# FNet mixing and a dropless mixture of experts on one core: the second block's weights requested ahead of both blocks' rows

## The chip, the core and the metric

The kernel runs on one NeuronCore of a Trainium2 chip. The engines are TensorE (PE in the profile, with its weight loads as PEld), VectorE (DVE), ScalarE (ACT), GpSimd (POOL) and SyncE (SP, which issues most DMAs). The metric is the device time of one execution in microseconds. The time before is the median of three executions.

## The reference

Two stages in a row, all in float32.

```python
# x: (8, 2496, 256)
X = np.fft.fft(np.fft.fft(x, axis=1), axis=2).real     # FNet mixing
t = X.reshape(8 * 2496, 256)                           # 19968 tokens
logits = t @ w_gate                                    # 8 experts
e = argmax(logits); g = softmax(logits)[e]             # one expert for each token
y[token] = relu(t[token] @ w1[e]) @ w2[e]              # 256 -> 1024 -> 256
out = g[:, None] * y                                   # every token is computed, none dropped
```

## The kernel before

**Mixing.** The sequence transform of a batch (2496 rows) is done as 104 x 24 points. `first(b)` folds the input tile `xq` on VectorE, multiplies it with the cosine and sine table on TensorE (`half1`, tile `s`), copies the result to `t1` on ScalarE and stores it to a DRAM buffer `Td` (L342). Behind each such store it calls `load` for the following batch (L289). `regroup(b, h)` reads `Td` back in another order (L354). `second(b)` makes the 24-point transform, the transform over the features and the gate's logits, and `route` finds each token's expert and its place in a DRAM buffer `Xs`, in which every expert has a region of its own.

**Scatter.** Twenty groups of 128 rows for each batch are written to `Xs` by indirect DMAs from GpSimd, one for each call of `send` (L470, put on record as L236). A row is 258 floats: 256 features, the token's number and its gate weight.

**Experts.** `todo` is the list of blocks in the order in which they are worked on. The first six blocks have rows of batch 0 alone: two of 256 rows, then four of 128. Which expert a block has, and where its rows start, is known only at run time: `plan` computes a table for each group of blocks (`tabs`), and SP reads the table into a register before it issues the block's DMAs (L531 for the rows, L544 for the expert).

- `fetch_weights` issues two DMAs of 1 MB each, `w1_sb` (L546) and `w2_sb` (L548). Each has three buffers. One of the three buffers of `w1_sb` holds the table `rt` at first, so two are free at the start.
- `fetch_rows` issues five DMAs: four of the features (L536) and a small one of the token numbers and gate weights (L540). They wait for all the scatters of the block's batches.
- `fetch_some(k, most)` keeps `xbs` (rows) and `got` (weights) filled up to three blocks ahead. In each turn of its loop it takes the next rows, if their batch is in `whole`, and then the weights of block `k + len(got)`, but it leaves the loop if that block's table is not in `tabs` yet.

Then a block is transposed on VectorE (`turn`, L584, tile `xT`), multiplied with `w1_sb` (tile `ph`), put through the ReLU, multiplied with `w2_sb` (tile `py`), scaled and scattered to the output. Later blocks use a form with seven half-size products in place of eight.

**Order.** Nothing is scheduled automatically: each engine executes its instructions in the order in which the Python program emits them. `experts` is a generator that yields while it has nothing to emit, and the main loop (L997 on) then emits steps of the mixing of batches 1 and 2, of `close(0)` (the planning) and of `send`. At the start of the first block (L777 to L787) `experts` waits for the first table, fetches the first block's weights (`fetch_some(0, 1)`, L780), yields once so that the main loop emits every scatter that is left and puts batch 0 into `whole`, fetches on (`fetch_some(0)`, L783), yields nine times, during which the main loop emits one step each of planning or mixing, and transposes block 0. `fetch_some(k)` in L788 is called for every block.

In SP's order before, from the first weights on, with the time of issue in the profiled execution: the weights of block 0 (70.20 and 70.75 us), the rows of block 0 (85.08 to 87.59), the rows of block 1 (88.38 to 91.27), the weights of block 1 (92.06 and 92.61), one `Td` store (93.06) and one `xq` load (93.53) of the nine steps, the rows of block 2 (94.91), the weights of block 2 (100.44 and later).

Of the kernel before, what the change touches and what calls it, by code (L numbers as in the profile page):

```python
# [160 lines left out]
def in_order():  # L161


    todo = []
    for b, now in enumerate(rounds()):
        parts = [[(b, size, last, i) for i in range(k)] for size, k, last in now]
        if b == B - 1:
            few, many = parts[-2:]
            sure, more = many[:SURE], many[SURE:]
            k = len(few)  # L170
            end = more[(len(more) + 1) // 2:]
            more = more[:len(more) - len(end)]
            rest = []
            for i in range(k):
                rest += few[i:i + 1] + sure[len(sure) * i // k:len(sure) * (i + 1) // k][:1]
                rest += more[i:i + 1]
                rest += sure[len(sure) * i // k:len(sure) * (i + 1) // k][1:]
            parts = parts[:-2] + [rest + end]
        todo += sum(parts, [])
    return todo  # L180
# [35 lines left out]
def kernel(ctx: ExitStack, tc, x, w_gate, w1, w2, out):  # L216
# [310 lines left out]
    def fetch_rows(b, size, tab, i, flat=None):  # L527


        n = size // 128  # L530
        row = nc.sync.value_load(tab[:, 0, i:i + 1], min_val=0, max_val=ROWS - size)  # L531
        if flat is None:
            xb = bp.tile([128, BIG // 128, W], F32, tag="xb", name="xb", bufs=3)
            flat = xb[:].rearrange("p t c -> p (t c)")
        for q in range(4):
            taken(nc.sync.dma_start(  # L536
                out=flat[32 * q:32 * q + 32, 0:2 * size].rearrange("p (j e) -> p j e", e=64),
                in_=Xs[ds(row, size), 64 * q:64 * q + 64].rearrange("(j k) e -> k j e", k=32)), b)
        meta = flat[:, 2 * size:2 * size + 2 * n].rearrange("p (t c) -> p t c", c=2)
        taken(nc.sync.dma_start(out=meta, in_=Xs[ds(row, size), D:].rearrange("(t p) c -> p t c", p=128)), b)  # L540
        return flat, meta

    def fetch_weights(tab, i):
        ev = nc.sync.value_load(tab[:, 1, i:i + 1], min_val=0, max_val=E - 1)  # L544
        w1_sb = bp.tile([128, 2, F], F32, tag="w1", name="w1_sb", bufs=3)
        nc.sync.dma_start(out=w1_sb[:], in_=w1[ds(ev, 1)].rearrange("o p c f -> p (o c) f"))  # L546
        w2_sb = bp.tile([128, FC, D], F32, tag="w2", name="w2_sb", bufs=3)
        nc.sync.dma_start(out=w2_sb[:], in_=w2[ds(ev, 1)].rearrange("o p c d -> p (o c) d"))  # L548
        return w1_sb, w2_sb
# [28 lines left out]
    def turn(b, size, xb):  # L578


        xT = bp.tile([128, 2, BIG], F32, tag="xT", name="xT", bufs=1)
        n = min(size, 256)
        for h in range(-(-size // 256)):
            vec.transpose(free(xT[:], 256 * h, [32, n // 32], [BIG, 2], [1, 32]),  # L584
                          free(xb, 512 * h, [64, n // 32], [1, 2], [2, 32]))
            odd = xT[:, 1, 256 * h:256 * h + n]
            act.activation(odd, odd, ACTF.Copy, scale=-1.0)  # L587
            yield xT
        if halved(b, size):
            th = size // 2  # L590
            xs = bp.tile([128, 3, th], F32, tag="xs", name="xs", bufs=1)
            r = right(xs, *(xT[:, c, k * th:(k + 1) * th] for c in range(2) for k in range(2)))
            yield r
# [136 lines left out]
    def experts(todo):  # L730
# [4 lines left out]
        xbs, got, xT, used, left, soon, final = [], [], None, None, None, None, {}  # L735
# [15 lines left out]
        def fetch_some(k, most=3):  # L751

            b, size, last, at = todo[-1]
            if "pads" in whole and not final:
                rows = sp.tile([128, NSL, W], F32, tag="rows", name="rows")
                for i in range(3):
                    b, size, last, at = todo[i - 3]
                    final[len(todo) - 3 + i] = fetch_rows(b, size, tabs[b, size, last], at,
                                                          rows[:, i:i + 1].rearrange("p t c -> p (t c)"))
            while max(len(got), len(xbs)) < min(most, len(todo) - k) or len(xbs) < len(got):  # L760
                n = len(xbs)
                b, size, last, at = todo[k + n]
                if k + n in final:
                    xbs.append(final[k + n])
                elif (b, size, last) in tabs and b in whole:
                    xbs.append(fetch_rows(b, size, tabs[b, size, last], at))
                elif n < len(got):
                    break
                b, size, last, at = todo[k + len(got)]
                if (b, size, last) not in tabs:  # L770
                    break
                if len(got) <= n:
                    got.append(fetch_weights(tabs[b, size, last], at))

        for k, (b, size, last, at) in enumerate(todo):
            n, m = size // 128, BIG // size
            if not k:  # L777
                while todo[0][:3] not in tabs:
                    yield 0, False
                fetch_some(0, 1)  # L780
                while b not in whole:
                    yield 0, True
                fetch_some(0)  # L783
                for _ in range(9):
                    yield 0, False
                for xT in turn(b, size, xbs[0][0]):
                    pass  # L787
# [177 lines left out]
    tabs, whole = {}, set()  # L965
    todo = in_order()
# [24 lines left out]
    for k, _ in enumerate(second(0)):  # L991
        if k % 2 == 0:
            next(early, None)
        send()
    work = experts(todo)
    steps = {b: mixed(b) for b in range(1, B)}
    for b in range(1, B):  # L997
# [83 lines left out]
```

## The time and the profile before

| what | value |
|---|---|
| median of three executions | 1260.61 us (1259.76 to 1261.67) |
| the profiled execution's own time | 1258.56 us |
| its span, first to last instruction | 1256.8 us |
| mean granted TensorE clock over the span | 0.976 of full speed |
| TensorE matmuls | 1208.1 us busy, 96% of the span |
| TensorE weight loads | 1076.3 us, 86% |
| VectorE, ScalarE, GpSimd | 60%, 34%, 36% |
| DMA | 249.79 MB, mean 199 GB/s over the span |

All times inside the execution count from the first instruction. About 1.8 us of the execution's own time lie outside the span. The page cuts the span into 40 slices of 31.4 us. Matmuls are pipelined and their ends are modelled, so a busy TensorE is one that has work, not one at its peak. The chain of waits follows the work that ended last backwards, step by step, to what released it. The table of DMA queues lists a hardware queue (q1, the DMAs that SP issues) and a software queue (q0, GpSimd's indirect DMAs); both are served by the same 16 DMA engines.

### The profile page before, as it was taken

How to read it: one execution, taken by the hardware profiler on the slowest of the kernel's cores; microseconds unless marked ns; L12 is line 12 of the kernel's file. 1: busy time of each engine (PE TensorE's matmuls, PEld its weight loads, DVE VectorE, ACT ScalarE, POOL GpSimd, SP SyncE). 2: the span in 40 equal slices, each digit the busy share in tenths (PEclk: the TensorE clock that was granted, in tenths of full speed). 3: DMA queues.
4: the chain of work that ended last, by engine and by line, in shares of the span. 5: the costliest groups of instructions: out<-in, count | busy, mean ns of one | idle time of the engine just before them, and what ended most of it. 6: DMA issues, size and time to landing. Idle time of an engine off the chain costs nothing.

```text
span 1256.8 us, 22295 instructions
## 1 busy us (share of the span) xinstructions
PE 1208.1 (96%) x7289; PEld 1076.3 (86%) x7289; DVE 759.6 (60%) x1804; ACT 431.3 (34%) x1167; POOL 447.5 (36%) x527
## 2 busy tenths in 40 slices
PE   5759999999999999999999999999999999999997
PEld 3648998777788899888988899889999999999996
DVE  3455434343456788566866578686888784444653
ACT  1424332333243433434343333442333332222222
POOL 0154527054117522472226603472364241111112
PEclk6869999999999999999999999999999999999998
DMA  8859899873548434673336435453347237878787
GB/s 235 261 174 350 308 317 311 221 237 122 154 153 263 151 110 163 184 234 116 102 124 211 138 96 162 138 180 101 106 139 206 94 105 284 277 285 284 280 292 284
DMA packets 163216, 249.79 MB, mean 199 GB/s; under 512 B 118601, under 2 KB 130227, under 8 KB 143516
## 3 DMA queue, kind: packets, MB, share of 16 engines
q1 hardware_dynamic: 146327, 203.28, 50.7%
q0 software_dynamic: 15888, 42.14, 9.1%
q10 hardware_dynamic: 885, 2.94, 0.7%
q8 instruction: 59, 0.97, 0.3%
q14 instruction: 57, 0.47, 0.1%
HBM read 194.91 MB, written 54.83 MB: 199 GB/s over the span
## 4 chain that ended last, share of the span: by engine, by line
PE 82%; DVE 9%; DMA 4%; ACT 2%; issue 2%; POOL 0%; SPq 0%; POOLq 0%; DVEq 0%; ACTq 0%
PE py L221 25%; PE ph L221 13%; PE a L221 11%; PE c L221 9%; PE p L221 6%; PE b L221 6%; PE d L221 5%; PE e L221 4%; PE s L221 3%; DMA xq<-in_x_dram 1%; DVE xT L584 1%; DMA Td<-t 1%; DVE y L684 1%; DMA Xs<-rows,pi 1%; DVE hT L639 1%
## 5 line engine op out<-in xcount | busy, mean ns | idle before, releaser
L236 POOL DMA_INDIRECT out_dram<-y,ro x163 | 161.4, 990 | 625.3 <-ACT y L680 301.3
L221 PE MATMUL py<-w_sb,hT 128*128 128x256 f32 x1504 | 339.5, 379 | 0.0
L221 PEld LDWEIGHTS py<-w_sb,hT 128*128 128x128 f32 x1504 | 281.4, 190 | 36.9 <-issue 1.0
L236 POOL DMA_INDIRECT Xs<-rows,pi x160 | 162.4, 1015 | 112.0 <-DVE rows L410 56.7
L221 PE MATMUL ph<-xT,w_sb 128*128 128x128 f32 (+2 forms) x992 | 171.1, 328 | 11.2 <-DVE xT L584 11.1
L221 PEld LDWEIGHTS ph<-xT,w_sb 128*128 128x128 f32 x992 | 136.3, 192 | 35.1 <-issue 16.8
L410 DVE SCALAR_TENSOR_TENSOR rows<-p,zs 128x129 f32<-128x129 f32 x160 | 48.9, 348 | 128.8 <-ACT lg L408 124.8
L221 PE MATMUL a<-xT,w_sb 128*128 128x256 f32 (+1 forms) x512 | 117.8, 357 | 0.0
L838 DVE TENSOR_SCALAR hT<-ph 128x512 f32<-128x512 f32 x43 | 29.7, 691 | 123.7 <-PE ph L221 63.7
L587 ACT ACTIVATE xT<-xT 128x256 f32<-128x256 f32 (+1 forms) x94 | 36.5, 388 | 179.2 <-DVE xT L584 140.8
L221 PEld LDWEIGHTS a<-xT,w_sb 128*128 128x128 f32 x512 | 88.6, 190 | 9.7
L892 ACT ACTIVATE y<-py,xb 128x256 f32<-128x256 f32 x94 | 44.6, 475 | 152.2 <-PE py L221 152.2
L636 DVE TENSOR_TENSOR hT<-hT,b 128x512 f32<-128x512 f32 x57 | 39.2, 688 | 75.7 <-PE b L221 50.0
L646 ACT ACTIVATE hT<-a 128x512 f32<-128x512 f32 x57 | 34.0, 597 | 134.1 <-PE a L221 131.1
L221 PE MATMUL s<-xq,w 104*112 104x256 f32 (+2 forms) x208 | 62.8, 425 | 16.3 <-DVE xq L297 12.1
L469 POOL CAST pi<-due 128x1 int32<-128x1 f32 x140 | 45.1, 322 | 65.5 <-ACT due L468 65.5
L221 PE MATMUL a<-w_sb,hT 128*128 128x128 f32 x528 | 66.0, 276 | 0.0
L221 PEld LDWEIGHTS a<-w_sb,hT 128*128 128x128 f32 x528 | 63.1, 192 | 0.7
L221 PEld LDWEIGHTS p<-table,t 120*128 120x128 f32 x352 | 53.6, 202 | 10.6 <-ACT t L372 2.8
L221 PE MATMUL c<-xT,ws 128*128 128x256 f32 (+1 forms) x256 | 60.3, 362 | 1.0 <-DVE hT L642 0.2
L221 PEld LDWEIGHTS s<-xq,w 104*112 104x112 f32 x208 | 38.5, 204 | 26.3 <-DVE xq L297 10.8
L584 DVE STREAM_TRANSPOSE xT<-xb 128x512 f32<-128x512 f32 (+1 forms) x91 | 56.2, 631 | 7.6 <-DMA xb<-Xs 7.6
(149 smaller groups left out, 2072.6 us busy)
## 6 DMA issues: line engine op xcount, KB each, us to landing
w_sb<-in_moe_w_dram SPq DMA_DIRECT2D x132, 1024.0 KB
xq<-in_x_dram SPq DMA_DIRECT2D x24, 896.0 KB
xb<-Xs SPq DMA_DIRECT2D x112, 128.0 KB
Td<-t SPq DMA_DIRECT2D x18, 448.0 KB
t<-Td SPq DMA_DIRECT2D x8, 768.0 KB
t<-Td SPq DMA_DIRECT2D x8, 640.0 KB
xb<-Xs SPq DMA_DIRECT2D x52, 64.0 KB
xb<-Xs SPq DMA_DIRECT2D x88, 32.0 KB
```

The costliest lines, as they stand in the source:

```text
L221: nc.tensor.matmul(o, lhsT=lhsT, rhs=rhs, start=start, stop=stop, **kw)
L236: return unordered(pool.indirect_dma_start(out=dst, out_offset=bass.IndirectOffsetOnAxis(ap=idx, axis=0), in_=rows, in_offset=None, bounds ...
L410: vec.scalar_tensor_tensor(rows[:, k + m, 0:NY], p3[:, 0:NY], zs[:, 0:1], zs[:, 1:], op0=ALU.add, op1=op)
L469: pool.tensor_copy(idx, due[:])
L584: vec.transpose(free(xT[:], 256 * h, [32, n // 32], [BIG, 2], [1, 32]), free(xb, 512 * h, [64, n // 32], [1, 2], [2, 32]))
L587: act.activation(odd, odd, ACTF.Copy, scale=-1.0)
L636: vec.tensor_tensor(h12, h11, b[:], op=add)
L639: vec.tensor_tensor(h21, h12, d[:], op=add)
L646: act.activation(h11, a[:], ACTF.Relu)
L684: vec.tensor_tensor(o, o, p[:], op=add)
L838: vec.tensor_scalar(o, ph[:], 0.0, None, op0=ALU.max)
L892: act.activation(y[:, i % 2], py[:], ACTF.Copy, scale=meta[:, i, 1:2])
```

## The change

One line is added behind the first `fetch_some` call.

```diff
                 while todo[0][:3] not in tabs:
                     yield 0, False
                 fetch_some(0, 1)
+                got.append(fetch_weights(tabs[todo[1][:3]], todo[1][3]))
                 while b not in whole:
                     yield 0, True
                 fetch_some(0)
```

Blocks 0 and 1 have the same table, which is there at this point. SP now issues the two weight DMAs of block 1 directly behind those of block 0, before it waits for the scatters. The numbers of DMAs and of buffers stay the same.

`got` is then one longer when `fetch_some(0)` is called in L783. Its loop takes the rows of block 0 and looks next at the table of block `0 + len(got)`, which is now block 2 and not block 1. That table is finished only within the nine steps that follow, so the loop is left there. The rows of block 1 are fetched by the next call (L788), together with the rows and the weights of block 2. SP's new order is: the weights of blocks 0 and 1, the rows of block 0, the `Td` store and the `xq` load, the rows of block 1, the rows of block 2, the weights of block 2. From there on it is the old one.

## The prediction

> **What bounds the kernel now.** I read the 40 slices first, then the waits of the stretch in which the change acts, then the chain, SP's issues and the DMA view there, and last TensorE's waits in all that follows. The slices say that TensorE is full from the fourth one on:
>
> ```profile
> PE   5759999999999999999999999999999999999997
> DMA  8859899873548434673336435453347237878787
> ```
>
> The third slice (62.8 to 94.3 us) holds the place of the change. Waits between 78 and 93 us (total, times, longest):
>
> ```profile
> PE ph L221 <- DVE xT L584: 11.1, 1, 11.1
> DVE xT L584 <- DMA xb<-Xs: 7.6, 1, 7.6
> ```
>
> TensorE stands still for 11.1 us, until block 0 is transposed, and the transpose waits for block 0's rows. The chain tells what the rows wait for (start, length):
>
> ```profile
> 82.36 2.48 DMA Xs<-rows,pi
> ...
> 86.69 1.98 DMA xb<-Xs
> ...
> 88.79 0.72 DVE xT L584
> 89.51 0.04 issue
> 89.55 3.66 PE ph L221 x8
> ```
>
> The last scatter of batch 0 is issued at 82.36 and lands at 84.84; then SP issues the rows (85.08), they land, are transposed, and TensorE starts at 89.55. So 89.55 - 84.84 = 4.71 us lie behind the last scatter's landing. The weights do not stand in this chain. SP's issues:
>
> ```profile
> 70.75 0.37 SPq L548 DMA_DIRECT2D w_sb<-in_moe_w_dram  x1
> 85.08 1.92 SPq L536 DMA_DIRECT2D xb<-Xs  x4
> 87.19 0.40 SPq L540 DMA_DIRECT2D xb<-Xs  x1
> 88.38 2.29 SPq L536 DMA_DIRECT2D xb<-Xs  x4
> 90.87 0.40 SPq L540 DMA_DIRECT2D xb<-Xs  x1
> 92.06 0.37 SPq L546 DMA_DIRECT2D w_sb<-in_moe_w_dram  x1
> ```
>
> The stages around it (length; busy us of PE, PEld, DVE, ACT, POOL with counts; clock, DMA share, GB/s):
>
> ```profile
> 76.00:78.00 2.00, 1.50 (x12) 1.42 (x13) 1.03 (x4) 1.09 (x6) 1.39 (x3) 1.00 0.99 392
> 78.00:80.00 2.00, 0.49 (x4) 0.27 (x3) 0.80 (x5) 0.65 (x3) 1.70 (x2) 1.00 0.79 305
> 80.00:82.00 2.00, 0.00 (x0) 0.00 (x0) 1.21 (x4) 0.00 (x0) 1.70 (x2) 1.00 0.19 68
> 92.00:94.00 2.00, 2.00 (x13) 1.79 (x11) 0.00 (x0) 0.75 (x2) 0.00 (x0) 0.76 0.53 75
> ```
>
> Block 0's weights fill the DMA engines until about 79 us; from 80 on they are nearly idle. In the DMA view of 79.3 to 85.0 only the software queue is left, and between 100 and 130 us, where the hardware queue is never empty, a scatter takes far longer to land (last number, median us):
>
> ```profile
> q0 software_dynamic: 213, 0.52, 25.7%
> Xs<-rows,pi POOLq DMA_INDIRECT x13, 7.0
> ```
>
> From 93 us to the end TensorE waits for no transfer at all. Its list has six entries, 4.9 us together, the largest being
>
> ```profile
> PE p L221 <- ACT t L372: 2.0, 4, 0.8
> PE p L221 <- ACT t L321: 1.2, 3, 0.7
> ```
>
> So whatever shifts the restart at 89.55 shifts the end by as much, and a transfer that comes sooner behind it has almost nothing to win.
>
> **What the Trainium skill says.** "DMA: Bandwidth & Descriptors", section "Issuing engines are not separate DMA queues": DMAs of SP, ScalarE and GpSimd run on the same 16 engines and interleave. The trace agrees: 2.48 us for the last scatter on quiet engines, 7.0 on full ones. Same page, "Queues, rings and completion order": each engine goes round-robin between its queues, packet by packet, so a scatter is not simply behind all the weights. The trace agrees in part: of the scatters issued in 70 to 86 us the median landed after 4.9 us, though block 0's weights were ahead. "TensorE: Matmul & The Clock Gate", Part 1: the clock is halved after an idle window of some 3.4 us and is full again after a busy one, and the windows run free of the program. The trace agrees: clock 0.50 at the restart, and 0.76 in 92 to 94 us puts the return at 93.0, 3.4 us after it.
>
> **The change part by part.**
>
> *Weights of block 1, moved forward.* Two DMAs of 1 MB. Between SP's last issue for a block's rows and its next weights lie 0.79 us (91.27 to 92.06), for the reading of the table. So they are issued at 71.12 + 0.79 = 71.9 and 72.5. SP has nothing else to do until the scatters have landed: its 1.7 us cost nothing here, and are saved at 91.3. Their buffers are free, and no hardware-queue traffic is left from earlier (the DMA view of 66 to 71 us lists none), so nothing holds them back. Who needs them is not waiting: block 1's first product is at 116.3, and before they had landed by 100.44, when SP's next weight issue got past its wait for them. **Gain on the path: none.**
>
> *What they meet.* Until 79.3 block 0's weights fill the engines in both versions. Then before there were 0.52 MB of scatters to move; now there are 0.52 + 2.10 = 2.62 MB. In 71.5 to 79.3 both queues together moved 346 GB/s, in 76 to 78 us 392; over 74 to 79, 1.85 MB in 5 us, 370. At 370 this is 7.1 us: all is through at 86.4 (86.0 at 392, 86.9 at 346). Scatters are a fifth of the bytes. Behind block 0's weights the view of 79.3 to 85.0 shows 0.4 us of full rate, the scatters that had stayed behind. I add the same, so the last scatter lands at 86.8 in place of 84.84: **2.0 us later.** Bounds: with an even share for the scatters it has its own 2.5 us plus a few packets' delay, 85.1, **0.3**; if the weights always go first, they alone need 2.10 MB at the 265 GB/s that the hardware queue got in 71.5 to 79.3 (2.07 MB in 7.8 us), until 87.2, and the 0.52 MB follow at 370 in 1.4 us, 88.6; the median of 7.0 us on full engines gives 82.36 + 7.0 = 89.4. So **up to 4.5.** I take neither end, since the weights run dry before 7.0 us are over.
>
> *GpSimd.* Twenty scatters, one each 1.28 us. Its DMAs signal on eight semaphores in turn, so the issue at 82.36 needs the landing of the one of 70.71. The longest landing of the trace up to 131 us is 8.4 us, which gives 79.1: the issues don't move. Beyond 11.6 us they would, a part of the slow case.
>
> *Rows of block 0.* Their issue waits for the last scatter; the weights are through by then or within half a microsecond. The 4.71 us stay.
>
> *Rows of block 1, behind the store and the load.* Five DMAs, moved from 88.4 behind one `Td` store (its data copied by 75.9) and one `xq` load (its buffer's last product ended at 74.5): 1.34 MB, 3.6 us at 370. Issued from about 92 to 95 and landed by 98 at the latest; the next transpose on VectorE is at 106.84. **Nothing**, 9 us of cover; without it, each us would be one on TensorE. The store and the load come some 3 us sooner, and the rows and weights of block 2 no later than before; behind them the order is the old one.
>
> *Relief.* 2.10 MB, 5.7 us of full rate, leave the stretch behind 93, which is full until past 130. TensorE waits for no transfer there. **At best 0.7 us** (its single wait in 99 to 103, for ScalarE, if that came from buffers), likely 0.
>
> *Clock.* TensorE is cold at the restart either way, for the first window that is busy throughout: 3.4 to 6.8 us, whatever the time of restart. In this profile it was 3.4, the least. A later restart in the same grid would stay cold until 96.4: a profile after may show up to 1.7 us more, a median over executions not.
>
> **Sum:** 2.0 + 0 + 0. Against the profiled execution's own time that is 1258.56 + 2.0 = 1260.6, with up to 1.7 for the clock's grid 1262.3. The median of the runs shown is 2.05 above that execution, so I put the same 2.0 on it: 1260.61 + 2.0 = **1262.6 us**.
>
> **The rivals.** (1) *The weights starve the scatters*: 3.7 to 4.5 us, 1265; slower. For it: 7.0 us of landing on full engines. Against: the weights run out at 86 to 87. It decides once the last scatter lands after 87.4. (2) *The scatters get their share*: 0.3 us, 1260.9. For it: round-robin; against: the landing of 4.9 us under only one block's weights. (3) *The relief counts*: the weights fill idle engines at little delay, and the freed 5.7 us behind 93 bring something that the waits don't show, half of it say: 1260.6 + 0.3 - 2.9 = 1258.0; against it, the list without transfers. (4) *The fetch isn't sooner*, held by a buffer or a slot: no difference, 1260.6; but all are free.
>
> **How the numbers follow.** 0.2%, 2.5 us, is about what a measurement of this kernel can tell from no change. My case, 1.2 to 2.9 us (1261.8 to 1263.5): 0.50. Rival 1: 0.27; rivals 2 and 4: 0.17; rival 3: 0.06. Slower: all but a little of rival 1 and three tenths of mine, 0.40. Faster: 0.06. Same: 0.54. The range takes in rivals 1 and 2 and 0.8 us for the spread of medians: 1260.0 to 1265.8.
>
> **What would show it.** In the profile after: SP's four weight issues at 70 to 73; a DMA share near 1 until 86; the chain still through the last scatter, with about 4.4 us to land in place of 2.48; rows at 87; TensorE restarting at 91.5 and its waits behind unchanged. It is wrong if the last scatter lands before 85.2 or after 87.8, if TensorE waits for block 1's rows near 107, or if the time falls.

## The result, and the profile after

| | before | after |
|---|---|---|
| median of 22 executions each | 1259.72 us (1255.78 to 1261.87) | 1261.53 us (1259.95 to 1265.02) |
| ratio after to before, 95% interval | | 1.0020 (1.0012 to 1.0027) |
| the profiled execution's own time | 1258.56 us | 1261.17 us |
| its span, mean granted clock | 1256.8 us, 0.976 | 1259.4 us, 0.977 |

The kernel became a little slower: 1.8 us between the medians, 2.5 us by the ratio (1.5 to 3.4). The interval lies above 1, but the effect is about the size of the 0.2% bound, and the forecast (+2.0 us on the median) is inside it. The 1262.6 us that it came to stood on a median of three executions of the kernel before (1260.61); 22 of them put that median 0.9 us lower.

The profile is read in the order of the prediction. The slices of after (busy tenths in 40 slices) show the old picture, with one tenth less in the first slice, ahead of the change, and in the third:

```profile
PE   4749999999999999999999999999999999999997
DMA  8877899763548535573336435453346328888887
```

Waits of after between 78 and 93 us (total, times, longest):

```profile
PE ph L221 <- DVE xT L584: 12.6, 1, 12.6
DVE xT L584 <- DMA xb<-Xs: 9.1, 1, 9.1
```

They are the same two waits, each 1.5 us longer (11.1 and 7.6 before). The chain of after through that stretch (start, length):

```profile
82.02 4.09 DMA Xs<-rows,pi
86.36 0.35 SPq L536
...
87.96 1.93 DMA xb<-Xs
89.98 0.72 DVE xT L584
90.74 3.78 PE ph L221 x8
```

The last scatter is issued 0.34 us *earlier* than before (82.02, not 82.36), but takes 4.09 us to land in place of 2.48. From landing (86.11) to restart (90.74) there are 4.63 us; before they were 4.71. So from the last scatter's issue to TensorE's restart it is 8.72 us in place of 7.19, which is 1.53 us more, all of it in that one landing. SP's issues in after:

```profile
70.43 0.37 SPq L548 DMA_DIRECT2D w_sb<-in_moe_w_dram  x1
71.59 0.34 SPq L546 DMA_DIRECT2D w_sb<-in_moe_w_dram  x1
72.11 0.33 SPq L548 DMA_DIRECT2D w_sb<-in_moe_w_dram  x1
86.36 1.92 SPq L536 DMA_DIRECT2D xb<-Xs  x4
...
91.89 2.12 SPq L536 DMA_DIRECT2D xb<-Xs  x4
...
95.42 3.62 SPq L536 DMA_DIRECT2D xb<-Xs  x4
...
100.38 0.36 SPq L546 DMA_DIRECT2D w_sb<-in_moe_w_dram  x1
```

The second weight pair is issued right behind the first; the rows of block 1 follow at 91.89. The stages of after (length; busy us of PE, PEld, DVE, ACT, POOL with counts; granted clock, DMA share, GB/s):

```profile
80.00:82.00 2.00, 0.00 (x0) 0.00 (x0) 0.87 (x2) 0.00 (x0) 1.72 (x1) 0.50 1.04 429
82.00:84.00 2.00, 0.00 (x0) 0.00 (x0) 0.00 (x0) 0.00 (x0) 0.97 (x1) 0.50 1.00 417
84.00:86.00 2.00, 0.00 (x0) 0.00 (x0) 0.00 (x0) 0.00 (x0) 0.00 (x0) 0.50 0.58 230
92.00:94.00 2.00, 2.00 (x6) 1.56 (x6) 0.00 (x0) 0.00 (x0) 0.00 (x0) 0.50 0.94 291
94.00:96.00 2.00, 2.00 (x10) 1.91 (x9) 0.00 (x0) 0.96 (x2) 0.00 (x0) 0.50 1.14 192
96.00:98.00 2.00, 2.00 (x10) 1.76 (x9) 0.61 (x2) 0.88 (x4) 0.00 (x0) 0.82 0.73 95
```

In 80 to 82 us the engines move 429 GB/s; before it was 68. They stay full until about 85. The clock column (third from the end) of the lower lines shows a second loss: the clock is still 0.50 in 92 to 96 us, and 0.82 in 96 to 98 puts its return at 96.7. Before, it returned at 93.0. The DMA view of after, 78 to 86 us (by queue: packets, MB, share of the 16 engines; then the issues with the median us to landing):

```profile
q1 hardware_dynamic: 295, 2.07, 62.9%
q0 software_dynamic: 342, 0.88, 27.9%
...
Xs<-rows,pi POOLq DMA_INDIRECT x4, 6.3
```

In before the same 8 us held 0.91 MB of the software queue and 0.06 MB of the hardware queue, and the scatters issued in it landed after 3.2 us in the median. The 2.07 MB are nearly all of block 1's two weight tiles. The last of their data is through at 85.01, the last packet of the scatters at 85.60, and the last scatter lands at 86.11. This last half microsecond is there without the weights too: in before the last packet of the scatters is through at 84.33, and the landing comes at 84.84.

Behind 95 us TensorE's waits in after are the old ones, again six entries with 4.9 us together:

```profile
PE p L221 <- ACT t L372: 2.0, 4, 0.8
PE p L221 <- ACT t L321: 1.2, 3, 0.7
```

Set side by side from the restart on, TensorE's weight loads in after have lost another 1.24 us by 4.7 us past the restart, and from there to the last product that distance never changes by more than 0.1 us. So what differs behind the restart up to the last product is the longer half clock: 5.98 us of it (90.74 to 96.72) in place of 3.42, at half speed worth 1.28 us.

### The profile page after: what moved, and what is told of

Read it like the earlier page. It is cut to its first block, busy times and chain, and to the rows that moved or that the text cites. A ratio compares the mean times of both kernels' runs of the same rounds, so it can differ in the third digit from the quotient of the medians.

```text
span 1259.4 us, 22295 instructions
## 1 busy us (share of the span) xinstructions
PE 1206.9 (96%) x7289; PEld 1076.0 (85%) x7289; DVE 759.6 (60%) x1804; ACT 431.8 (34%) x1167; POOL 448.6 (36%) x527
## 4 chain that ended last, share of the span: by engine, by line
PE 81%; DVE 9%; DMA 4%; ACT 2%; issue 2%; SPq 1%; POOL 0%; POOLq 0%; DVEq 0%; ACTq 0%
PE py L221 24%; PE ph L221 12%; PE a L221 11%; PE c L221 9%; PE p L221 6%; PE b L221 6%; PE d L221 5%; PE e L221 4%; PE s L221 3%; DVE xT L584 1%; DMA Td<-t 1%; DVE y L684 1%; DMA Xs<-rows,pi 1%; DMA w_sb<-in_moe_w_dram 1%; DMA xq<-in_x_dram 1%
## 5 line engine op out<-in xcount | busy, mean ns | idle before, releaser
L221 PE MATMUL p<-table,t 120*128 120x120 f32 (+1 forms) x352 | 57.5, 289 | 2.3 <-ACT t L372 2.0
```

The costliest lines, as they stand in the source:

```text
L221: nc.tensor.matmul(o, lhsT=lhsT, rhs=rhs, start=start, stop=stop, **kw)
```

## The experiments

**Theory S:** the early weights delay the last scatter's landing, wherever the rows of block 1 stand. **Rival O:** the order of the rows is what costs. Two further questions came up: how the delay grows with the bytes, and whether the half clock is part of the change (rival C in the texts below). The kernels of one group ran on one chip, each group beside its own runs of the kernel before: e1 to e4 (before there 1258.91 us), e5 to e8 (1273.75), e9 to e12 (1259.09).

**The rows alone moved** (to before, in L783: block 1's rows and weights are then fetched by the call in L788):

```diff
-                fetch_some(0)
+                xbs.append(fetch_rows(*todo[0][:2], tabs[todo[0][:3]], todo[0][3]))
```

> Only the other half of the change: the weights of block 1 stay where they were, behind the rows of block 1, but those rows are fetched only behind the nine steps (behind the Td store and the xq load). If the scatters are what the change delays (theory S), the last scatter again lands some 2.5 us after its issue, TensorE restarts as in the kernel before and the time is that of before, within 0.5 us. If the new place of block 1's rows costs the time (rival O), it is slower than before by 1.5 to 2.5 us and TensorE waits for a transpose near 107 us.

Measured: 1258.85 us, ratio 1.0000 (0.9990 to 1.0009). The chain of that kernel:

```profile
83.97 2.36 DMA Xs<-rows,pi
...
88.19 1.90 DMA xb<-Xs
...
90.97 3.78 PE ph L221 x8
```

The landing takes 2.36 us and the restart comes 7.00 us after the issue. Moving the rows behind the store and the load costs nothing that shows: the interval leaves room for 1.1 to 1.3 us either way.

**The weights alone moved**, the rows in their old place (to before):

```diff
                 fetch_some(0, 1)
+                got.append(fetch_weights(tabs[todo[1][:3]], todo[1][3]))
                 while b not in whole:
                     yield 0, True
-                fetch_some(0)
+                xbs.append(fetch_rows(*todo[0][:2], tabs[todo[0][:3]], todo[0][3]))
+                xbs.append(fetch_rows(*todo[1][:2], tabs[todo[1][:3]], todo[1][3]))
```

> Only the weights of block 1 are moved: SP's order is weights 0, weights 1, rows 0, rows 1, then the Td store and the xq load as before. Theory S: the last scatter takes 4.1 us to land in place of 2.5, TensorE's idle time before the first block is 12.6 us in place of 11.1, and the time is that of the changed kernel, 1.5 to 2.5 us above before. Rival O: the time is that of before.

Measured: 1261.90 us, ratio 1.0021 (1.0013 to 1.0029). The chain of that kernel:

```profile
82.19 4.07 DMA Xs<-rows,pi
...
88.11 1.91 DMA xb<-Xs
...
90.87 3.78 PE ph L221 x8
```

The landing is as long as in after (4.07), the restart 8.68 us behind the issue. The whole slowdown is there without the change of the rows' order: rival O falls.

**The weights of block 1 between the two blocks' rows** (to before):

```diff
-                fetch_some(0)
+                xbs.append(fetch_rows(*todo[0][:2], tabs[todo[0][:3]], todo[0][3]))
+                got.append(fetch_weights(tabs[todo[1][:3]], todo[1][3]))
+                xbs.append(fetch_rows(*todo[1][:2], tabs[todo[1][:3]], todo[1][3]))
```

> The weights of block 1 ahead of block 1's rows but behind block 0's, so that they are issued when all scatters have landed. Theory S: the last scatter lands in 2.5 us, TensorE restarts as before, the time is that of before within 0.5 us; the weights' 2 MB now stand in front of block 1's rows, which still land well before the transpose at 107 us. If it is the mere earlier use of the engines behind 88 us that matters (relief or harm later), it would differ from before by more than 1 us.

Measured: 1259.41 us, ratio 1.0005 (0.9996 to 1.0013). The chain of that kernel:

```profile
82.73 2.45 DMA Xs<-rows,pi
...
89.90 3.74 PE ph L221 x8
```

With the weights behind the scatters' landing the delay is gone: 2.45 us, and 7.17 from issue to restart.

**The changed kernel once more**, for the spread on this chip:

> The changed kernel once more, on the chip and in the rounds of the three others: the ratio to before again near 1.002 (1.5 to 2.5 us). Its profile has another phase of TensorE's clock window: the last scatter's landing and the 12.6 us of idle TensorE should come again within 0.3 us (theory S), while the time of half clock behind the restart may lie anywhere from 3.4 to 6.8 us (6.0 in the first profile, 3.4 in that of before). If the half clock is again near 6 us in this kernel and near 3.4 in those that restart as before, the clock is a part of the loss and not chance (rival C).

Measured: 1262.15 us, ratio 1.0026 (1.0017 to 1.0035). The chain again has the long landing:

```profile
81.08 3.85 DMA Xs<-rows,pi
...
89.61 3.78 PE ph L221 x8
```

**Half of the early bytes.** Only `w1_sb` of block 1 goes early; `w2_sb` follows behind the rows of block 1 (to before; `fetch_half` is `fetch_weights` cut in two):

```diff
                 fetch_some(0, 1)
+                early = fetch_half(None, tabs[todo[1][:3]], todo[1][3])
                 while b not in whole:
                     yield 0, True
-                fetch_some(0)
+                xbs.append(fetch_rows(*todo[0][:2], tabs[todo[0][:3]], todo[0][3]))
+                xbs.append(fetch_rows(*todo[1][:2], tabs[todo[1][:3]], todo[1][3]))
+                got.append(fetch_half(early, tabs[todo[1][:3]], todo[1][3]))
```

> Half the dose: only w1_sb of block 1 (1 MB) is fetched ahead of the scatters' wait; its w2_sb follows behind block 1's rows. If the delay comes from bytes that have to be through before the last scatter (the prediction's sum), the extra 1 MB at 400 GB/s ends 2.6 us sooner than 2 MB and the last scatter is hardly late: its landing takes 2.5 to 2.9 us and the time is within 0.7 us of before. If the scatters fall behind as soon as any second transfer follows, it is most of 4.1 us.

Measured: 1272.19 us, ratio 0.9987 (0.9973 to 1.0000). This does not test the theory. In this profile TensorE stands still three times ahead of the restart, 8.2 us in all, without waiting for anything that the profile shows. Waits of that kernel between 60 and 97 us:

```profile
PE p L221 <- issue: 8.2, 3, 5.3
```

So products ran until 90.8, VectorE folded behind them, and the restart (94.14) came from that side; the landing, at about 86.0 (SP issued the rows at 86.23), had been done for long. The same kernel on the third chip:

> The half dose again, on a chip where TensorE has no stretches of 3 to 5 us without instructions ahead of the restart, as it had in the first try. 1 MB at 400 GB/s is through 2.6 us sooner than 2 MB. If the bytes have to be through, the last scatter lands 2.5 to 2.9 us after its issue and the time is within 0.7 us of before; if any second transfer is enough to hold the scatters back, it takes most of 4.1 us.

Measured: 1260.10 us, ratio 1.0005 (0.9997 to 1.0014). The chain of that run:

```profile
79.97 4.55 DMA Xs<-rows,pi
...
89.05 3.52 PE ph L221 x8
```

The landing is delayed as in after, 4.55 us, though the weights are through at 83.10. But GpSimd had issued its twenty scatters in 26.27 us from first to last, where before, after, e2 and e4 took 27.1 to 27.2, and so the last one landed sooner. (Three of the twenty issues took longer than the rest here, the 11th, 12th and 16th; in before and after four did, the 9th, 10th, 14th and 19th. Why is not known; e12 below went as e11.) From the first scatter's issue to the restart it is 35.35 us here, 34.36 in before and 35.82 in after: the half load costs 1.0 us of the 1.5. The medians say 1.0 us as well, but the ratio's interval takes in no difference. About half a microsecond of it may not be the weights' doing: the landing comes 1.1 us behind the last packet of the scatters (83.46), in before, after, e1 to e4 and e12 0.4 to 0.7. So the long landing speaks for the second of the two expectations, and how the delay grows below 2 MB is not settled.

**Twice the early bytes** (to after; two transfers of 1 MB more, right behind the others, into a tile that is free at that time; nothing reads them):

```diff
                 got.append(fetch_weights(tabs[todo[1][:3]], todo[1][3]))
+                more = bp.tile([128, FC, BIG], F32, tag="hT", name="hT", bufs=1)
+                for i in range(2):
+                    nc.sync.dma_start(out=more[:, 4 * i:4 * i + 4].rearrange("p a b -> p (a b)"),
+                                      in_=w1[i:i + 1].rearrange("o p c f -> p (o c f)"))
```

> Double the dose: behind the weights of block 1 two more transfers of 1 MB (two experts' w1, into the buffer of hT, which nothing uses yet) are issued, so 4 MB stand behind block 0's weights; nothing reads them. If the scatters simply wait for all bytes, the last one lands 5 us later than in the changed kernel, near 91 us, and the time rises to 6 or 7 us above before. If they keep a share of the engines once these are full, the last scatter takes about the 7 us that scatters take later on full engines and lands near 89 us: 4 us above before.

Measured on the second chip: 1277.24 us, ratio 1.0026 (1.0010 to 1.0041), with the last scatter landing after 6.35 us. The comparison with before is spoilt by the waits named above. On the third chip:

> The double dose again on such a chip (two transfers of 1 MB that nothing reads, behind the weights of block 1). In the first try the last scatter took 6.4 us to land and then the rows of block 0 took 6.0 us in place of 2.0, being behind the extra transfers in SP's queue. If that is how it goes on: the scatter lands near 88.5, the transpose starts near 95, TensorE idles some 17 us, and the time is 5 to 7 us above before. If the scatters wait for all bytes, they land near 91.

Measured: 1265.41 us (six runs), ratio 1.0046 (1.0032 to 1.0060). The chain of that run:

```profile
79.50 6.05 DMA Xs<-rows,pi
...
87.42 6.58 DMA xb<-Xs
...
94.89 3.78 PE ph L221 x8
```

From the first scatter's issue to the restart it is now 41.66 us, 7.3 more than in before. The landing grows to 6.05 us, which ends at 85.55, while the hardware queue's bytes last until 91.7: the scatter keeps a share and does not wait for all the bytes ahead. And a second wait appears: the rows of block 0, issued by SP from 85.80 on, come late: the last of their four feature DMAs takes 6.58 us to land in place of 2, since they stand in SP's own queue behind the weights that are not through. In after this second wait is absent: the weights have run dry at 85.01, ahead of the rows' issue at 86.36.

**The clock filled up.** If TensorE's idle time ahead of the restart were filled with products whose results are not used, it would keep its clock, and what then still separates the two kernels would be the landing alone (80 products in before, 92 in after, ahead of the transpose of block 0):

```diff
+                for i in range(80):
+                    pw = pse.tile([128, D], F32, tag="bd"[i % 2], name="py")
+                    mm(pw[:], ones[:], bc(ones[:], 1, 2))
```

> The kernel before with 80 matmuls of ones (bf16, 128x256[...]) on TensorE in the idle stretch ahead of the first block, so that its clock is not halved at the restart. They end near 88 us, ahead of the restart at 89.5. Rival C and the clock's part of theory S: the first eight products of block 0 take 1.9 us in place of 3.7 and the time falls by half of the half-clock time, 1.7 to 3.4 us. If the clock doesn't matter, no difference.

> The changed kernel with 92 such matmuls in its longer idle stretch. With the clock full at the restart in both, the difference to the same filling in the kernel before is the scatters' delay alone: 1.3 to 1.6 us by theory S. If it stays at 2.5 us, the clock had no part in the difference; if it vanishes, the clock was all of it.

Measured: 1278.99 us, ratio 1.0043 (1.0025 to 1.0060), and 1281.43, ratio 1.0057 (1.0037 to 1.0076). Both fill too much. The chain of the first one:

```profile
91.14 12.91 PE py L221 x80
104.05 1.80 PE ph L221 x8
```

A filling product took 0.16 us, more than I had sized the filling for, and the filling itself set the restart. With 58 and 66 products on the third chip:

> The kernel before with 58 matmuls of ones in the idle stretch ahead of the first block. In the first try (80 of them) they took 0.163 us each[...], 13.1 us in all, more than the 11.1 us of idle time, so the filling itself delayed the restart. 58 take 9.5 us and end about 1.5 us ahead of the restart, so TensorE's clock is full at the restart. If the clock's part is real, the first eight products take 1.9 us in place of 3.7 and the time falls by 1.7 to 3.4 us; if not, no difference.

> The changed kernel with 66 such matmuls (10.8 us in 12.5 us of idle time). With the clock full at the restart in both, the difference to the same filling in the kernel before is the scatters' delay alone, 1.3 to 1.6 us by theory S; the changed kernel so filled comes out below the kernel before by about 1 us. If the difference stays at 2.5 us, the clock had no part in it; if it vanishes, the clock was all of it.

Measured: 1258.46 us, ratio 0.9992 (0.9982 to 1.0003), and 1260.94, ratio 1.0016 (1.0004 to 1.0029). TensorE's timeline of the filled kernel before (start, length, then the idle time and its releaser in brackets):

```profile
77.08 9.48 PE L221 MATMUL py<-ones 128*128 128x256 bf16 x58
88.64 2.01 PE L221 MATMUL ph<-xT,w_sb 128*128 128x256 f32 x8 [2.08 <-DVE xT L584]
```

The clock stayed full there: the first eight products take 2.01 us in place of 3.66. Counted from the restart, TensorE is 1.65 us ahead of before by 4 us past it, and still so at 1050 us of the profile. Yet only 0.6 us of that lead was left at its last product. In between, weight loads of late blocks waited for transposes, which stood on VectorE behind work on weight tiles (L567) that had just landed (at 1162.04, for one, after 6.26 us of waiting for that DMA). Waits of TensorE's weight loads in that kernel between 1000 and 1240 us:

```profile
PEld a L221 <- DVE xT L584: 1.5, 4, 0.7
```

Before has no such wait. The end gave back what was left, and more, since the last `y` waited longer for an output scatter. Waits of that kernel from 1245 us on:

```profile
ACT y L895 <- DMA out_dram<-y,ro: 2.8, 1, 2.8
```

In before this wait is 1.1 us. In the filled changed kernel the clock fell all the same; its stages:

```profile
90.00:92.00 2.00, 2.00 (x7) 1.62 (x8) 0.00 (x0) 0.38 (x1) 0.00 (x0) 0.77 0.83 254
92.00:94.00 2.00, 2.00 (x9) 1.82 (x9) 0.00 (x0) 0.94 (x2) 0.00 (x0) 0.50 0.95 276
```

0.77 in 90 to 92 us is the moment at which it drops (91.06), 1.08 us behind the restart (89.98), which had 1.95 us of idle time ahead of it. So the pair was not equally warm, and it does not show what the clock contributes. It does show the longer landing once more, on the third chip: 2.46 us in e9 and 4.17 in e10.

**Side by side**, from the profiled executions (us; the ratio is that of all runs):

| kernel | landing of the last scatter | its issue to restart | half clock behind the restart | restart to end of span | ratio |
|---|---|---|---|---|---|
| before | 2.48 | 7.19 | 3.42 | 1167.2 | 1 |
| rows moved alone (e1) | 2.36 | 7.00 | 4.35 | 1168.1 | 1.0000 |
| weights between (e3) | 2.45 | 7.17 | 3.56 | 1167.5 | 1.0005 |
| after | 4.09 | 8.72 | 5.98 | 1168.7 | 1.0020 |
| weights moved alone (e2) | 4.07 | 8.68 | 5.41 | 1168.6 | 1.0021 |
| after again (e4) | 3.85 | 8.53 | 5.34 | 1169.1 | 1.0026 |

**What is shown:** the early weights make the landing 1.4 to 1.7 us longer (3.85 to 4.09 against 2.36 to 2.48), and with it the time from the last scatter's issue to the restart (8.53 to 8.72 against 7.00 to 7.19), with the rows in either place; without the early weights neither happens. That the scatter loses this time at the DMA engines, which are full in that stretch, and not in memory behind them, is argued from their share (1.00 to 1.04); no run separates the two.

**What stays open:** the measured ratios of after, e2 and e4 amount to 2.5, 2.6 and 3.3 us, about 1 us more than this delay. Each interval alone comes close to the delay (its lower end is 1.5, 1.6 and 2.1 us), but the 35 runs of e2 and e4 have a mean 2.9 us above that of the 77 runs of before, e1 and e3 on the same chip, with a standard error of 0.3 if the runs count as independent. So there seems to be more than the delay, and two things could be it.

The first is the clock. In the profiles of after, e2 and e4 the half clock lasted 5.3 to 6.0 us in place of 3.4 to 4.4, which at half speed is 0.5 to 1.3 us, of the right size. But this is one execution of each kernel, and in e12, which restarts 5 us later than before, it lasted 3.97 us (94.89 to 98.86), so a late restart does not by itself bring a long half clock. Over those runs on one chip the mean granted clock was 0.9801 in the 35 and 0.9803 in the 77, a difference below 0.0003 with a standard error of 0.0009. The missing microsecond would need some 0.0008 on top of the 0.0006 that 1.5 us more of idle time at half clock bring, so this neither confirms it nor excludes it.

The second is the late wait for weights that e9 showed. In e4 it was as large, and TensorE fell back by another 0.9 us between 1000 us and its last product, which with the half clock makes up the 1169.1 us of the table. Its line between 1000 and 1240 us:

```profile
PEld a L221 <- DVE xT L584: 1.4, 3, 0.7
```

It was 0.5 us in e2, 0.3 in e3, 1.8 in e10, and none in before, after and e1. It comes with and without the change, and one profile of each kernel does not tell whether the change makes it more frequent.

## Why the prediction was right, point by point

The mechanism was right, and the one number of its sum was too large: 2.0 us, where the delay is 1.5. That the measured change (1.8 us between the medians, 2.5 by the ratio) came out close to 2.0 is in part luck, since about 1 us of it stood in no term of the sum.

- **The bound** was as described: the restart of TensorE behind block 0's transpose sets the end. The restart comes 1.19 us later in the profile of after (90.74, not 89.55), 1.24 us are lost to the clock behind it, and the span is 2.6 us longer.
- **Weights moved forward:** issued at 71.59 and 72.11, where 71.9 and 72.5 were worked out; the execution is 0.3 us early as a whole there. No buffer held them. Nothing gained on the path, as said.
- **What they meet:** right in mechanism, mis-sized in the sum. Issue to landing was put at 4.4 us and measured 4.09, so the delay was 1.6 us at the landing and 1.5 at the restart, not 2.0 (bounds given: 0.3 to 4.5). The term at fault is the time until all bytes are through: 86.4, which is 4.0 us after the last scatter's issue, and measured 85.60, which is 3.6. The sum had 2.62 MB at 370 GB/s. In after 2.55 MB moved from 79.0 (0.3 early) to 85.6, at 387 GB/s in the mean. The DMA view of that stretch:

```profile
DMA packets 552, 2.55 MB, mean 387 GB/s; under 512 B 146, under 2 KB 146, under 8 KB 336
q1 hardware_dynamic: 248, 1.77, 64.1%
q0 software_dynamic: 304, 0.78, 30.0%
```

The bytes also lie otherwise: 0.33 MB of block 1's weights had moved earlier, and 0.26 MB more of the scatters had stayed behind. The remainder of 0.4 us was nearly right in size (0.5), but not for the reason given: it is not a rest of scatters to be moved, but time between the last packet and the landing, and before has it too.
- **The passages of the Trainium skill** hold. "DMA: Bandwidth & Descriptors", "Issuing engines are not separate DMA queues": GpSimd's scatter is slowed by what SP issued (4.09 against 2.48 us). Same page, "Queues, rings and completion order": with 4 MB ahead the scatter landed 6.1 us before the hardware queue was through (85.55, 91.7), so the queues do take turns, while the rows in SP's own queue had to wait (6.58 us in place of 2). What was said of the clock holds with a reservation (see the last section).
- **GpSimd:** its last issue did not move back (82.02 against 82.36). The spacing given, 1.28 us, is that of most issues; with the four longer ones the mean is 1.43. **Rows of block 0:** 4.63 us from landing to restart, 4.71 given.
- **Rows of block 1:** issued from 91.89 to 94.6, as worked out (92 to 95), and free of cost (e1). The transpose of block 1 waits for nothing; it is at 109.28 instead of 106.84, later by what TensorE is late. A small wait was not foreseen: the four issues of block 2's rows took 3.62 us in place of 2.10, behind the `xq` load; nobody waits for it, and block 2's weights leave at 100.38, as before (100.44).
- **Relief:** none, as said. The engines moved 42 GB/s in 98 to 100 us where before they moved 303, and no wait of TensorE behind 95 us became shorter. That TensorE waits for no transfer behind the restart is right for before and after, but the margin is small: in e4, e9 and e10 its weight loads waited 1.4 to 1.8 us behind late weights.
- **Clock:** for the profile up to 1.7 us was allowed, and 1.28 came. The 3.4 us named as the least were undercut once (3.13 in e11, 89.05 to 92.18). For the median nothing was put on the clock; whether that was right stays open.
- **The rivals.** The scatters were not starved (landed at 86.11, ahead of the 87.4 from which that case decides), and they did not get an even share at no cost either. The fetch was sooner. No relief came.

## What to carry to other kernels

A transfer that nobody waits for is not free where a short transfer on the critical path has to land while it runs: look for what must land last in that stretch, and add up the bytes until then. Place the bulk behind that landing (here between the two blocks' rows, at no measurable cost). It is not enough that it runs dry before the landing: in after it did (85.01 against 86.11), and the landing was still 1.6 us longer. Once it outlasts the landing, what follows in the same queue waits as well (e12). An earlier fetch can only pay if some wait in the profile is for that fetch, and here there was none.

## What was not expected of the hardware

- The half clock: 1.95 us of idle time between the filling and the restart led to a drop (e10), while 2.08 us in e9 did not. The Trainium skill, "TensorE: Matmul & The Clock Gate", Part 1, speaks of idle windows of about 3.4 us; these two runs fit it only if such a window may be partly busy, and if it matters how the idle time falls across the grid of windows. The clock changes of one trace lie whole multiples of 3.41 us apart, which gives the grid: in e10 the 1.95 us (88.04 to 89.98) lie within one window (87.65 to 91.06), while in e9 a border at 87.46 splits the 2.08 us into 0.90 and 1.18.
- A gain on TensorE can vanish on the way: in e9 1.65 us of lead behind the restart became 0.6 at the last product, by late waits for weights, and nothing was left of it at the end of the span, behind the landing of an output scatter (2.8 us of waiting in place of 1.1).
- The kernel before took 1259 to 1260 us beside after, e1 to e4 and e9 to e12, but 1273.75 on the chip of e5 to e8. In the profiles taken there TensorE had stretches of up to 5.3 us in which it waited for nothing that the profile shows. Before has one too, of 3.3 us, so whether they make up the difference is not shown.
